# Attention and two MoE layers on one core: for the first batch, the softmax division moves behind the product with V

## The chip, the cores and the metric

The kernel runs on one core of one Trainium2 chip. The metric is the device time of one execution in microseconds; the time before is the median of three runs.

## What is computed

Four batches of eight heads of causal attention with a decay, 576 positions and 64 channels per head; then an MoE-like layer (a maximum over three products, and an output product), then a second one with a rational gate:

```python
scores = scale * np.matmul(q, k.transpose(0, 1, 3, 2))
scores = np.where(causal, -1000000000.0, scores + decay)
scores = scores - np.max(scores, axis=-1, keepdims=True)
attn = np.exp(scores)
attn = attn / (np.sum(attn, axis=-1, keepdims=True) + 1e-09)
x = np.matmul(attn, v)            # then heads side by side: (2304, 512)
h = np.maximum(np.maximum(x @ w1, x @ w2), x @ w3)
x2 = h @ w_out
...                               # second layer: x2 @ w_in, gate, @ w_out
```

The expert weights arrive as 64-bit floats and are turned into pairs of 32-bit halves (high and low) on the chip.

## The kernel before

Heads are handled two at a time: a `Pair` is two heads of one batch. The 576 queries are cut into five blocks (64, then four of 128) in two groups, g = 0 (the first 320 queries) and g = 1 (the last 256). The first batch is made of eight pairs, n = 0 to 3 for group 0 and n = 4 to 7 for group 1; from n = 8 on a pair has both groups. A `Unit` is one head and one group of a pair, and is named n_h_g: `e_7_1_1` is a tile of pair 7, head 1, group 1.

A unit goes through three steps of a software pipeline, one slot apart. In `scores` TensorE multiplies q and k (L343, or L345 and L346), VectorE adds the mask and takes the row maximum (L347), and ScalarE takes the exponential and its row sums (L353). `normalise` then adds 1e-9 to the sums and inverts them on VectorE (L358, L359), and GpSimd multiplies every block of probabilities by its reciprocal (L362). In `turn`, one slot later, TensorE transposes the probabilities (L382) and ScalarE copies them out of PSUM (L384). In `attend`, another slot later and once per pair, TensorE multiplies by V (L398); ScalarE and VectorE split the result into a high and a low part `x` (L405, L406).

The first MoE layer (`moe1_h`, L430 to L443, and `moe1_o`, L455 to L461) is cut into small pieces, which `fill` puts between the steps of the attention. A piece of `moe1_h` is twelve matmuls and one maximum `m`, whose tiles come from the pool `mpool` under the tag `mx`, which has three buffers. In the names, `h_0_0_4` is a product for batch 0, group 0, fourth chunk of channels counted from 0; `x2p` are the output products. The conversion of the weights (`convert`: L169 to L171 on ScalarE and VectorE, L172 and L175 on VectorE, L178 on ScalarE, L179 on GpSimd) is put in between by the same routine; it makes the tiles `cv_w`, `w1h`, `w1l` and their like. For the first four pairs TensorE also runs two matmuls on a constant before each use of a PSUM bank (`exercised`, L84).

A scheduler fixes the order on each engine when the program is built: it takes whatever its own model of the time holds ready, in the order in which the code was written. On the chip each engine runs its list in that order and waits where a semaphore says so.

Of the kernel before, what the change touches and what calls it, by code (L numbers as in the profile page):

```python
# [8 lines left out]
F32 = mybir.dt.float32  # L9
F32R = mybir.dt.float32r  # L10
I32 = mybir.dt.int32
AF = mybir.ActivationFunctionType
ALU = mybir.AluOpType
# [6 lines left out]
Q0 = [0, 64, 192, 320, 448]  # L20
# [4 lines left out]
GQ = [(0, 320), (320, 576)]  # L25
GBLK = [(0, 1, 2), (3, 4)]
# [6 lines left out]
GBANK = [[(1, 2), (0,)], [(1, 2), (3, 4), (0,)]]  # L33
# [4 lines left out]
def kernel(  # L38
    ctx: ExitStack, tc: tile.TileContext, q, k, v, f, w1, w2, w3, w_out, m2_in, m2_out, m2_a, m2_b, out
):  # L40
    nc = tc.nc
    B, H, S, D = q.shape
# [3 lines left out]
    P = 128  # L46
# [3 lines left out]
    NPAIR = H // 2  # L50
    NB = len(Q0)

    def r32(ap):
        return ap.bitcast(F32)
# [7 lines left out]
    mpool = ctx.enter_context(tc.tile_pool(name="mpool", bufs=1, side="left"))  # L62
    wpool = ctx.enter_context(tc.tile_pool(name="wpool", bufs=1, side="left"))
    apool_cm = ExitStack()
    apool = apool_cm.enter_context(tc.tile_pool(name="apool", bufs=1, side="right"))
    ps_cm = ExitStack()
    ps_s = ps_cm.enter_context(tc.tile_pool(name="ps_s", bufs=2, space=PSUM))
    ps_t = ps_cm.enter_context(tc.tile_pool(name="ps_t", bufs=3, space=PSUM))
# [4 lines left out]
    ident = const.tile([P, P], F32, name="ident")  # L73
# [6 lines left out]
    def exercised(bank, n):  # L80

        if n < 4:
            for _ in range(WARM):
                nc.tensor.matmul(bank, warm[:, 0], wide, start=True, stop=True)  # L84
        return bank
# [27 lines left out]


    LOOK, WHOLE, PRE = 2, 6, 2
    CONV2, EARLY = (32, 0.25), 12
    kqs = {}

# [105 lines left out]
    xt = {}  # L224
    x2d = dram.tile([P, NDC, 2, NT], F32R, name="x2d")

    def pinned(ld):
        tc.keep_in_program_order(ld)
# [12 lines left out]
    class Pair:  # L241


        def __init__(self, n, b, hp, groups):
            self.n, self.b, self.hp, self.groups = n, b, hp, groups
            self.ng = groups[-1] + 1
            self.nk = GBLK[groups[-1]][-1] + 1
            self.ik = [(2 * n + h) % NKB for h in range(2)]
            self.iq = [[(2 * n + h) % m for h in range(2)] for m in NQB]
            self.pt = {}  # L250
            self.whole = n < WHOLE
            self.iqf = [(2 * n + h) % 4 for h in range(2)]

        def load(self):
# [58 lines left out]
    class Unit:  # L313
# [5 lines left out]

        def begin(self):  # L320
            self.st = apool.tile([P, 9], F32, name=f"st_{self.nm}", tag="st", bufs=3)
            self.rs = apool.tile([P, 2, 3], F32, name=f"rs_{self.nm}", tag="rs", bufs=3)

        def scores(self, i):
            p, h, g = self.pair, self.h, self.g
# [29 lines left out]
        def normalise(self):  # L355
            blks = GBLK[self.g]
            n = len(blks)
            nc.vector.tensor_scalar_add(self.rs[:, 0, :n], self.rs[:, 0, :n], 1.0e-9)  # L358
            nc.vector.reciprocal(self.rs[:, 1, :n], self.rs[:, 0, :n])  # L359
            for j, i in enumerate(blks):  # L360
                e = self.e[i]
                nc.gpsimd.tensor_scalar(e, e, self.rs[:, 1, j : j + 1], 0.0, op0=ALU.mult, op1=ALU.add)  # L362

        def turn(self, bank):

            g, p = self.g, self.pair
            hi = GQ[g][1]
            if g not in p.pt:
                p.pt[g] = pts[g]
            pt = p.pt[g][:, self.h]  # L370
            chunks = GBANK[g][bank]
            tp = exercised(ps_t.tile([P, 512], F32, name=f"tp{bank}_{self.nm}", tag="t"), self.pair.n)
            base = GCH[g][chunks[0]][0]
            n = 0
            for c in chunks:
                col, q0 = GCH[g][c]
                kr = Q1[c] - Q0[c]
                for i in GBLK[g]:
                    if i < c:
                        continue  # L380
                    dst = col - base + Q0[i] - q0
                    nc.tensor.transpose(tp[:kr, dst : dst + P], self.e[i][:, Q0[c] : Q1[c]], ident)  # L382
                n += hi - q0
            nc.scalar.activation(pt[:kr, base : base + n], tp[:kr, :n], AF.Copy)  # L384

        def attend(self):

            p, h, g = self.pair, self.h, self.g
            if h == 0:
                return  # L390
            lo, hi = GQ[g]
            w = hi - lo
            ot = exercised(ps_o.tile([P, 512], F32, name=f"o_{self.nm}", tag="o"), p.n)
            order = list(GCH[g].items())
            with tc.high_priority():
                for j, (c, (col, q0)) in enumerate(order):
                    for i in (1, 0):
                        mm = nc.tensor.matmul(  # L398
                            ot[SIDES[i][0], q0 - lo : w], p.v[:, c, i], p.pt[g][:, i, col : col + hi - q0],
                            start=(j == 0), stop=(j == len(order) - 1),  # L400
                        )
                        if (j, i) != (0, 1):
                            pinned(mm)
            x = mpool.tile([P, 2, w], F32R, name=f"x_{self.nm}", tag=f"x{g}", bufs=(6, 8)[g])
            nc.scalar.activation(x[:, 0], ot[:, :w], AF.Copy)  # L405
            nc.vector.tensor_tensor(x[:, 1], ot[:, :w], r32(x[:, 0]), op=ALU.subtract)  # L406
            xt[p.b, p.hp, g] = x
# [131 lines left out]
    for step in range(len(slots) + 2):  # L539
        u = slots[step] if step < len(slots) else None  # L540
        t = slots[step - 1] if 0 <= step - 1 < len(slots) else None
        o = slots[step - 2] if 0 <= step - 2 < len(slots) else None
        prep, NPRE = [], 0
        if u is not None and u.pair.n + 1 < len(pairs):
            n = u.pair.n + 1
# [252 lines left out]
```

## Time and profile before

| | us |
|---|---|
| median of three runs (range) | 968.99 (967.96 to 969.51) |
| the profiled execution | 970.9 |
| its span, first to last instruction | 969.1 |

| engine | busy, us | share of the span |
|---|---|---|
| TensorE (PE) | 943.1 | 97% |
| weight loads (PEld) | 829.9 | 86% |
| VectorE (DVE) | 739.6 | 76% |
| ScalarE (ACT) | 623.8 | 64% |
| GpSimd (POOL) | 252.4 | 26% |

Shares are means over stages with different limits. The attention of the first batch takes the first 160 us; the conversion of the first layer's weights lies in the same stretch. A busy PE is not PE at its peak: the ends of matmuls are modelled, and a waiting matmul is partly counted. So the profile is read by stretches.

### The profile page before, as it was taken

Reading aid. Unit: us, or ns where it says so; the run is one execution under the profiler, and the core shown is the slowest. Engines: PE = TensorE matmul, PEld = TensorE weight load, DVE = VectorE, ACT = ScalarE, POOL = GpSimd, SP = SyncE. Lnnn points to the kernel's source line nnn. Section 1 sums busy time; section 2 is a strip of 40 time slices with the busy share of each in tenths; the row PEclk is TensorE's granted clock in tenths of the full one; section 3 lists DMA queues with packets and bytes.
Section 4 is the critical chain, followed back from the end, with each engine's and each line's share of the span. In section 5 each row is a group of like instructions: output and inputs, shape, how many; then the busy total and the mean of one; then the engine's idle time right before and its main releaser. Section 6 shows DMA issues by size and latency. Waiting matters only on the chain.

```text
span 969.1 us, 16846 instructions
## 1 busy us (share of the span) xinstructions
PE 943.1 (97%) x5780; PEld 829.9 (86%) x5780; DVE 739.6 (76%) x1756; ACT 623.8 (64%) x1457; POOL 252.4 (26%) x408
## 2 busy tenths in 40 slices
PE   7998999999999999999999999999999999999998
PEld 6767889998998988999999978888888888999997
DVE  5789985557777777534397949988888988899997
ACT  5875666667667666646454548767666766677775
POOL 2646553445454545425133400000000000000000
PEclk9978999999999999999999999999999999999999
DMA  6685233124446445230145477011002101100000
GB/s 160 159 236 153 64 83 89 43 63 119 140 131 205 133 136 174 58 94 1 57 140 185 132 253 269 1 44 43 1 1 66 44 1 46 64 1 1 34 1 33
DMA packets 125621, 88.52 MB, mean 91 GB/s; under 512 B 74448, under 2 KB 110304, under 8 KB 125536
## 3 DMA queue, kind: packets, MB, share of 16 engines
q1 hardware_dynamic: 125536, 87.45, 30.4%
q8 instruction: 46, 0.75, 0.4%
q14 instruction: 39, 0.32, 0.1%
HBM read 64.73 MB, written 22.69 MB: 90 GB/s over the span
## 4 chain that ended last, share of the span: by engine, by line
PE 70%; DVE 14%; DMA 6%; ACT 4%; issue 3%; POOL 2%; SPq 1%; ACTq 0%; POOLq 0%; DVEq 0%
PE oo L721 7%; PE oo L722 7%; PE oo L720 7%; PE hq L671 6%; PE hq L673 6%; PE hq L672 6%; PE tp L382 4%; PE h L430 4%; PE o L398 4%; PE h L431 4%; PE h L432 4%; PE x2p L455 2%; DMA raw_wi<-in_moe_w_in_dram 2%; PE x2p L456 2%; PE x2p L457 2%
## 5 line engine op out<-in xcount | busy, mean ns | idle before, releaser
L430 PE MATMUL h<-x,w1h 128*128 128x320 f32 (+1 forms) x576 | 176.6, 307 | 3.1 <-ACT m L435 2.2
L431 PE MATMUL h<-x,w1h 128*128 128x320 f32 (+1 forms) x576 | 172.1, 299 | 0.0
L432 PE MATMUL h<-x,w1l 128*128 128x320 f32 (+1 forms) x576 | 171.2, 298 | 0.0
L430 PEld LDWEIGHTS h<-x,w1h 128*128 128x128 f32 x576 | 109.4, 190 | 7.0 <-ACT m L435 3.0
L362 POOL TENSOR_SCALAR e<-e,rs 128x64 f32<-128x64 f32 (+4 forms) x160 | 87.7, 563 | 106.4 <-DVE rs L359 91.5
L353 ACT ACTIVATE e<-e,st 128x64 f32<-128x64 f32 (+4 forms) x160 | 89.1, 557 | 37.8 <-DVE st L347 36.0
L721 PE MATMUL oo<-wp,gh 128*128 128x512 f32 x288 | 112.9, 392 | 0.0
L720 PE MATMUL oo<-wp,gh 128*128 128x512 f32 x288 | 112.5, 390 | 0.0
L431 PEld LDWEIGHTS h<-x,w1h 128*128 128x128 f32 x576 | 109.5, 190 | 0.4 <-issue 0.2
L432 PEld LDWEIGHTS h<-x,w1l 128*128 128x128 f32 x576 | 109.2, 190 | 0.0
L722 PE MATMUL oo<-wp,gl 128*128 128x512 f32 x288 | 108.8, 392 | 0.0
L680 ACT ACTIVATE s<-hq 128x512 f32<-128x512 f32 (+1 forms) x80 | 44.3, 554 | 97.4 <-PE hq L673 97.4
L347 DVE CUSTOM_DVE_ANT_0 e<-s,mask 128x320 f32<-128x320 f32 (+3 forms) x160 | 67.2, 433 | 37.9 <-PE s L346 24.0
L384 ACT ACTIVATE pt<-tp 128x384 f32<-128x384 f32 (+3 forms) x160 | 69.8, 469 | 19.2 <-PE tp L382 17.4
L683 DVE SCALAR_TENSOR_TENSOR s<-s,ab,u 128x512 f32<-128x512 f32 (+1 forms) x80 | 55.7, 697 | 32.1 <-ACT u L681 31.9
L382 PE MATMUL tp<-ident,e 128*128 128x128 f32 (+1 forms) x480 | 78.0, 280 | 1.3 <-DVE k2s L275 0.6
L673 PE MATMUL hq<-x,wil 128*128 128x512 f32 (+1 forms) x192 | 70.4, 367 | 0.0
L671 PE MATMUL hq<-x,wih 128*128 128x512 f32 (+1 forms) x192 | 70.4, 367 | 0.0
L672 PE MATMUL hq<-x,wih 128*128 128x512 f32 (+1 forms) x192 | 70.3, 366 | 0.0
L722 PEld LDWEIGHTS oo<-wp,gl 128*128 128x128 f32 x288 | 54.1, 188 | 11.7
L720 PEld LDWEIGHTS oo<-wp,gh 128*128 128x128 f32 x288 | 54.2, 188 | 11.0
L721 PEld LDWEIGHTS oo<-wp,gh 128*128 128x128 f32 x288 | 54.1, 188 | 10.9
(129 smaller groups left out, 2433.6 us busy)
## 6 DMA issues: line engine op xcount, KB each, us to landing
raw_w<-in_moe_w_dram SPq DMA_DIRECT2D x18, 512.0 KB
raw_wp<-in_moe_w_out_dram SPq DMA_DIRECT2D x32, 256.0 KB
wpd<-wp SPq DMA_DIRECT2D x32, 256.0 KB
raw_wi<-in_moe_w_in_dram SPq DMA_DIRECT2D x32, 256.0 KB
wp<-wpd SPq DMA_DIRECT2D x10, 768.0 KB
x2d<-xo SPq DMA_DIRECT2D x16, 320.0 KB
out_dram<-ob SPq DMA_DIRECT2D x18, 256.0 KB
kn<-in_k_dram SPq DMA_DIRECT2D x32, 128.0 KB
```

Source lines behind the costliest of these rows:

```text
L353: nc.scalar.activation(e[:nr], e[:nr], AF.Exp, bias=m, scale=-1.0, accum_out=l)
L362: nc.gpsimd.tensor_scalar(e, e, self.rs[:, 1, j : j + 1], 0.0, op0=ALU.mult, op1=ALU.add)
L382: nc.tensor.transpose(tp[:kr, dst : dst + P], self.e[i][:, Q0[c] : Q1[c]], ident)
L430: nc.tensor.matmul(hp_[:, :w], wh[:, j, dc], xs[dc][:, 1], start=(dc == NDC - 1), stop=False)
L431: nc.tensor.matmul(hp_[:, :w], wh[:, j, dc], xs[dc][:, 0], start=False, stop=False)
L432: nc.tensor.matmul(hp_[:, :w], wl[:, j, dc], xs[dc][:, 0], start=False, stop=(dc == 0))
L671: nc.tensor.matmul(hp_[:, :w], wih[:, dc, fs], xh, start=(dc == 0), stop=False)
L672: nc.tensor.matmul(hp_[:, :w], wih[:, dc, fs], xl, start=False, stop=False)
L673: nc.tensor.matmul(hp_[:, :w], wil[:, dc, fs], xh, start=False, stop=(dc == NDC - 1))
L720: nc.tensor.matmul(o, g[0][:, ts_], wh_, start=(fc == 0), stop=False)
L721: nc.tensor.matmul(o, g[0][:, ts_], wl_, start=False, stop=False)
L722: nc.tensor.matmul(o, g[1][:, ts_], wh_, start=False, stop=(fc == NF2 - 1))
```

## The change

For the pairs of the first batch (n < `LATE`, which is 8) `normalise` no longer touches the probabilities. After the second head of a pair it adds 1e-9 and inverts the sums of both heads at once, and one GpSimd instruction spreads the reciprocals over a tile `rx` (64 equal columns per head and block). At the end of `turn` TensorE transposes `rx` block by block into a PSUM tile `rb`, and ScalarE copies that to `rn`, so that the reciprocals lie along the columns of the output. `attend` multiplies the output by `rn` on VectorE, and splits the product instead of the output itself. `rx` takes buffers of `e` tiles that the group doesn't use; `rn` takes a buffer of the tag `mx`.

```diff
+    LATE = NPAIR * 2
...
+            if self.pair.late:
+                if self.h == 1:
+                    rs = self.pair.rs
+                    nc.vector.tensor_scalar_add(rs[:, 0, :, :n], rs[:, 0, :, :n], 1.0e-9)
+                    nc.vector.reciprocal(rs[:, 1, :, :n], rs[:, 0, :, :n])
+                    rx = apool.tile([P, n, 2, D], F32, name=f"rx_{self.nm}", tag=("e3_", "e2_")[self.g] + str(self.pair.hp % 2))
+                    self.pair.rx = rx
+                    r = rs[:, 1, :, :n].rearrange("p h j -> p j h").unsqueeze(3).to_broadcast([P, n, 2, D])
+                    nc.gpsimd.tensor_scalar(rx, r, 1.0, 0.0, op0=ALU.mult, op1=ALU.add)
+                return
             nc.vector.tensor_scalar_add(self.rs[:, 0, :n], self.rs[:, 0, :n], 1.0e-9)
...
             nc.scalar.activation(pt[:kr, base : base + n], tp[:kr, :n], AF.Copy)
+            if p.late and self.h == 1 and bank == len(GBANK[g]) - 1:
+                lo, w = GQ[g][0], GQ[g][1] - GQ[g][0]
+                rb = ps_t.tile([P, 512], F32, name=f"rb_{self.nm}", tag="t")
+                for j, i in enumerate(GBLK[g]):
+                    nc.tensor.transpose(
+                        rb[:, Q0[i] - lo : Q0[i] - lo + P], p.rx[:, j].rearrange("p h d -> p (h d)"), ident
+                    )
+                p.rb = mpool.tile([P, 320], F32, name=f"rn_{self.nm}", tag="mx", bufs=3)
+                nc.scalar.activation(p.rb[:, :w], rb[:, :w], AF.Copy)
...
+            if p.late:
+                xn = p.rb
+                nc.vector.tensor_tensor(xn[:, :w], ot[:, :w], xn[:, :w], op=ALU.mult)
+                nc.scalar.activation(x[:, 0], xn[:, :w], AF.Copy)
+                nc.vector.tensor_tensor(x[:, 1], xn[:, :w], r32(x[:, 0]), op=ALU.subtract)
+                return
             nc.scalar.activation(x[:, 0], ot[:, :w], AF.Copy)
```

The new instructions give the scheduler another order. Two places show it. The first is TensorE's list around the unit 7_0_1 (`s` are score matmuls, `h` those of the first layer, `o` the product with V). Before, the last piece of the chunk `h_0_0_4` ends just ahead of the first scores of that unit:

```order
L431 MATMUL h_0_0_4_1805<-x_1_0_516,w1h_852 128x320
L432 MATMUL h_0_0_4_1805<-x_1_0_516,w1l_853 128x320
L430 MATMUL h_0_0_4_1805<-x_1_0_369,w1h_852 128x320
L431 MATMUL h_0_0_4_1805<-x_1_0_369,w1h_852 128x320
L432 MATMUL h_0_0_4_1805<-x_1_0_369,w1l_853 128x320
L345 MATMUL s_0_7_0_1_1483<-k1s_1334,q1s_1401 128x448
L346 MATMUL s_0_7_0_1_1483<-k2s_1335,q2s_1402 128x448
```

In the changed kernel the second piece of the same chunk begins only behind the scores of 8_1_0, the transposes `rb` of pair 7 and its product with V, with the scores of 8_0_1 begun:

```order
L407 MATMUL rb_1_1_1671<-ident,rx_1_1_1642 128x128 x2
L353 MATMUL s_0_8_1_0_1774<-k1s_1089,q1s_1625 128x320
L354 MATMUL s_0_8_1_0_1774<-k2s_1090,q2s_1626 128x320
L425 MATMUL o_1_1_1719<-pt_124,v_1422 64x256 x8
L425 MATMUL o_1_1_1719<-pt_124,v_1422 64x128 x2
L353 MATMUL s_0_8_0_1_1851<-k1s_1084,q1s_1153 128x448
L354 MATMUL s_0_8_0_1_1851<-k2s_1085,q2s_1154 128x448
L464 MATMUL h_0_0_4_1779<-x_1_0_836,w1h_848 128x320
```

So the pieces of the first layer stand later among the attention: ahead of the first scores of unit 8_1_1 there are 306 of its matmuls before (216 `h` of group 0, 72 `x2p`, 18 `h` of group 1) and 192 after. All other matmuls ahead of that place are the same in number, but for the 20 added transposes. Ahead of the scores of 13_0_0 the first layer's matmuls are again equal in number.

The second place is GpSimd's list in group 1. Before, each unit has two instructions on the probabilities between the low halves of the weights:

```order
L179 TENSOR_TENSOR w1l_674<-cv_w_2_675,w1h_673 128x512
L362 TENSOR_SCALAR e_4_0_1_783<-e_4_0_1_783,rs_0_1_782 128x448
L362 TENSOR_SCALAR e_4_0_1_798<-e_4_0_1_798,rs_0_1_782 128x576
L179 TENSOR_TENSOR w1l_674<-cv_w_2_708,w1h_673 128x512
L179 TENSOR_TENSOR w1l_674<-cv_w_2_725,w1h_673 128x512
L362 TENSOR_SCALAR e_4_1_1_888<-e_4_1_1_888,rs_1_1_887 128x448
L362 TENSOR_SCALAR e_4_1_1_903<-e_4_1_1_903,rs_1_1_887 128x576
L179 TENSOR_TENSOR w1l_752<-cv_w_3_753,w1h_751 128x512
```

In the changed kernel one instruction on the reciprocals stands for both units of a pair:

```order
L180 TENSOR_TENSOR w1l_669<-cv_w_2_702,w1h_668 128x512
L180 TENSOR_TENSOR w1l_669<-cv_w_2_719,w1h_668 128x512
L180 TENSOR_TENSOR w1l_745<-cv_w_3_746,w1h_744 128x512
L374 TENSOR_SCALAR rx_1_1_933<-rs_0_1_781 128x256
L180 TENSOR_TENSOR w1l_745<-cv_w_3_789,w1h_744 128x512
L180 TENSOR_TENSOR w1l_745<-cv_w_3_812,w1h_744 128x512
L374 TENSOR_SCALAR rx_1_1_1172<-rs_0_1_990 128x256
```

In the whole first batch 40 GpSimd instructions go and 8 come.

## Rows read from the trace of the kernel before

**Rows 1.** Windows: stretch, length, busy by engine (instructions), granted clock, DMA share, GB/s.

```profile
24.00:53.00 29.00, 28.49 (x166) 21.66 (x167) 20.19 (x66) 24.06 (x69) 17.20 (x24) 1.00 0.63 159
53.00:97.00 44.00, 38.99 (x196) 29.05 (x195) 41.24 (x86) 27.98 (x65) 25.62 (x25) 0.81 0.70 199
97.00:143.00 46.00, 41.27 (x287) 37.03 (x286) 42.37 (x111) 30.75 (x80) 26.66 (x38) 0.98 0.26 66
143.00:161.00 18.00, 18.00 (x125) 16.90 (x125) 7.82 (x31) 9.90 (x29) 4.79 (x12) 0.87 0.38 111
161.00:253.00 92.00, 90.92 (x738) 83.04 (x737) 55.93 (x206) 64.83 (x190) 43.34 (x84) 1.00 0.32 82
```

**Rows 2.** Timeline of VectorE around unit 8_1_1: start, duration, instruction.

```profile
155.41 0.42 DVE L406 TENSOR_TENSOR x<-o,x 128x256 fp32r<-128x256 f32 x1 [0.85 <-ACT x L405]
...
160.70 0.61 DVE L347 CUSTOM_DVE_ANT_0 e<-s,mask 128x448 f32<-128x448 f32 x1
```

**Rows 3.** Timeline of TensorE: two of the first layer's matmuls in a row.

```profile
79.81 0.31 PE L430 MATMUL h<-x,w1h 128*128 128x320 f32 x1
79.95 0.31 PE L431 MATMUL h<-x,w1h 128*128 128x320 f32 x1
```

**Rows 4.** Windows of line 362 alone: stretch, length, GpSimd busy (instructions), clock, DMA.

```profile
53.00:97.00 44.00, 6.67 (x8) 0.81 0.70 199
97.00:143.00 46.00, 6.00 (x8) 0.98 0.26 66
```

**Rows 5.** Groups by form, VectorE, 53 to 143 us: count, busy us, mean ns, idle before.

```profile
L175 DVE SCALAR_TENSOR_TENSOR cv_w<-raw_w,cv_w 128x512 int32<-128x512 int32 x12 | 11.4, 953 | 0.1
L172 DVE SCALAR_TENSOR_TENSOR cv_w<-raw_w,cv_w 128x512 int32<-128x512 int32 x12 | 9.8, 819 | 0.2
L175 DVE SCALAR_TENSOR_TENSOR cv_wo<-raw_wo,cv_wo 128x256 int32<-128x256 int32 x12 | 7.0, 586 | 0.2
...
L172 DVE SCALAR_TENSOR_TENSOR cv_wo<-raw_wo,cv_wo 128x256 int32<-128x256 int32 x12 | 6.0, 510 | 0.1
...
L170 DVE TENSOR_SCALAR cv_wo<-cv_wo 128x256 f32<-128x256 f32 x12 | 5.3, 448 | 0.8 <-ACT cv_wo L169 0.8
L171 DVE TENSOR_SCALAR cv_wo<-cv_wo 128x256 int32<-128x256 int32 x12 | 5.0, 426 | 0.1
```

**Rows 6.** Timeline of VectorE: the same forms where GpSimd stands still.

```profile
59.81 0.68 DVE L172 SCALAR_TENSOR_TENSOR cv_w<-raw_w,cv_w 128x512 int32<-128x512 int32 x1
...
113.91 0.42 DVE L175 SCALAR_TENSOR_TENSOR cv_wo<-raw_wo,cv_wo 128x256 int32<-128x256 int32 x1
114.25 0.28 DVE L170 TENSOR_SCALAR cv_wo<-cv_wo 128x256 f32<-128x256 f32 x1
114.57 0.29 DVE L171 TENSOR_SCALAR cv_wo<-cv_wo 128x256 int32<-128x256 int32 x1
```

**Rows 7.** Timelines of VectorE and of GpSimd at 58 us.

```profile
58.33 1.56 DVE L175 SCALAR_TENSOR_TENSOR cv_w<-raw_w,cv_w 128x512 int32<-128x512 int32 x1
...
58.06 1.27 POOL L179 TENSOR_TENSOR w1l<-cv_w,w1h 128x512 fp32r<-128x512 f32 x1 [5.44 <-ACT w1h L178]
```

**Rows 8.** Timelines of VectorE and of GpSimd at 28 us.

```profile
28.83 0.49 DVE L406 TENSOR_TENSOR x<-o,x 128x320 fp32r<-128x320 f32 x1
...
27.38 2.54 POOL L179 TENSOR_TENSOR w1l<-cv_w,w1h 128x512 fp32r<-128x512 f32 x2
```

**Rows 9.** Timeline of TensorE: three transposes and what follows them.

```profile
33.74 0.49 PE L297 MATMUL tk<-ident,kn 128*128 128x128 f32 x3
33.99 0.71 PE L84 MATMUL s<-warm 128*128 128x512 f32 x2
```

**Rows 10.** Windows, columns as in rows 1: the stretch around 230 us.

```profile
218.00:242.00 24.00, 22.92 (x177) 20.32 (x176) 16.80 (x59) 17.97 (x57) 12.17 (x22) 1.00 0.45 121
```

**Rows 11.** Product with V twice: TensorE's timeline at 74 us, the chain of waits at 152 us.

```profile
74.17 4.11 PE L398 MATMUL o<-pt,v 128*64 128x256 f32 x20 [0.83 <-DVE x L406]
...
152.85 2.10 PE o L398 x20
```

More of the change, by code (lines that the diff above doesn't have):

```diff
@@ L251, in __init__ @@
             self.whole = n < WHOLE
+            self.late = n < LATE
             self.iqf = [(2 * n + h) % 4 for h in range(2)]
@@ L321, in begin @@
             self.st = apool.tile([P, 9], F32, name=f"st_{self.nm}", tag="st", bufs=3)
-            self.rs = apool.tile([P, 2, 3], F32, name=f"rs_{self.nm}", tag="rs", bufs=3)
+            p = self.pair
+            if not p.late:
+                self.rs = apool.tile([P, 2, 3], F32, name=f"rs_{self.nm}", tag="rs", bufs=3)
+                return
+            if self.h == 0:
+                p.rs = apool.tile([P, 2, 2, 3], F32, name=f"rs_{self.nm}", tag="rsd", bufs=2)
+            self.rs = p.rs[:, :, self.h]
         def scores(self, i):
@@ L404, in attend @@
             x = mpool.tile([P, 2, w], F32R, name=f"x_{self.nm}", tag=f"x{g}", bufs=(6, 8)[g])
+            xt[p.b, p.hp, g] = x
+            if p.late:
[3 more added lines that the diff above has]
+                nc.vector.tensor_tensor(x[:, 1], xn[:, :w], r32(x[:, 0]), op=ALU.subtract)
+                return
             nc.scalar.activation(x[:, 0], ot[:, :w], AF.Copy)
```

## The prediction

> **What bounds the kernel now.** I read the windows by stage first [rows 1], then who is idle in each. From 24 to 53 us TensorE is busy 28.49 of 29 us and VectorE only 20.19: there the pairs of the first batch run at TensorE's pace, the constant matmuls of L84 included, and taking work off GpSimd or VectorE buys nothing. From 53 to 143 us it is the other way round. VectorE is busy 41.24 of 44 and 42.37 of 46 us, because the weights are converted there; TensorE has gaps, and its granted clock is 0.81 in the first of the two stretches, so part of that stretch ran at 1.2 GHz, not 2.4. From 143 to 161 us TensorE is busy 18.00 of 18 us and VectorE 7.82: now VectorE waits. From 161 us on TensorE is busy to within about a hundredth. So in the first 143 us VectorE decides from 53 us on, and later the amount of work that TensorE still has to do.
>
> That gives the way to count. I take as a mark the first score reduction of unit 8_1_1, at 160.70 us [rows 2]. From there on TensorE bounds, and by the scores of 13_0_0 both orders have done the same pieces of the first layer. The change in the total is the change in the time of the mark, plus the matmuls that the new order still owes at the mark, less idle time of TensorE that these owed matmuls fill afterwards.
>
> **The change part by part.**
>
> *Work on VectorE ahead of the mark.* The counts of the two orders differ there as follows. Eight multiplications with the reciprocals come: four of 320 columns at 0.49 us [rows 8] (the same shapes from PSUM) and four of 256 at 0.42 [rows 2], 3.6 us. Of the small additions and reciprocals, 30 become 16; at an estimated 0.16 us each, from the smallest VectorE operation that stands unstretched (0.28 for 256 columns [rows 6]) taken down for their few columns, that is 2.3 us less. Six operations of the first layer (two maxima, four splits) now stand behind the mark, and they have the shape of L406 at 0.49 us [rows 8]: 3.0 us less. Together -1.7 us. The conversions ahead of the mark are the same in number.
>
> *GpSimd's share of the stretching.* VectorE's conversions are slower beside GpSimd. At 58.33 us an L175 lasted 1.56 us while GpSimd's L179 ran from 58.06 for 1.27 [rows 7]; alone such a form takes 0.68 [rows 6] (L172 of the same shape). Over 53 to 143 us the excess is, as the means of rows 5 less the single times of rows 6 [rows 5, 6]: 12 x (0.953 - 0.68) = 3.3 and 12 x (0.819 - 0.68) = 1.7 for the large ones, 12 x (0.586 - 0.42) = 2.0, 12 x (0.510 - 0.42) = 1.1, 12 x (0.448 - 0.28) = 2.0 and 12 x (0.426 - 0.29) = 1.6 for the small ones, 11.7 us in all. GpSimd is busy 25.62 + 26.66 = 52.3 us there [rows 1], of which L362 has 12.7 [rows 4]; five of the new instructions come in, at an estimated 0.6 us each (L362 has 0.8 us for its mean of 512 columns [rows 4], and they have 256 or 384), 3 us. So 9.7 of 52.3 us go, 18.5%, and with them 18.5% of the excess: -2.2 us. The bounds are 0 (the rest of GpSimd's work moves up and stands in the way instead) and -9.7 (all of it was in VectorE's way). The value is near the first, since most of the stretching stands beside L179, which stays.
>
> *VectorE's idle time before the mark.* From 143 to 161 us VectorE idles 10.2 us behind TensorE [rows 1]. TensorE owes less there in the new order, so most of this closes: 54 of the first layer's matmuls stand between the scores of 8_0_0 and of 8_1_1 before, 36 after, while VectorE has some 3 us of work more between the two. I take -7.5 us; the bounds are -3 (the latency of score, maximum, exponential and transpose stays) and -10.2.
>
> The mark then comes at 160.7 - 1.7 - 2.2 - 7.5 = 149.3 us.
>
> *What TensorE owes at the mark.* 306 less 192 is 114 matmuls of 128x320, which follow each other every 0.147 us (79.81, 79.95 and on [rows 3]): +16.8 us. They are on the path, because TensorE has no idle time to speak of from 143 us on. This is the largest term. It comes from `rn`: it takes its turn in the three `mx` buffers, and a later maximum of the first layer gets that buffer only when the pair's output is split. Before, the first layer ran ahead of the attention and filled TensorE while VectorE converted weights; now it cannot run ahead.
>
> *Added transposes.* Three take 33.99 - 33.74 = 0.25 us [rows 9]. Nine fall into the stretch to 53 us where TensorE bounds: +0.7 us. The other eleven lie under VectorE's time; without that cover they would cost 0.9 us. ScalarE's two added copies per pair are covered as well: it is busy 27.98 of 44 us [rows 1]. A transpose `rb` makes TensorE wait for GpSimd, as the transposes of the probabilities did; queued behind it are the next scores and the product with V. `rx` sits in buffers of `e` tiles: the third block of 8_1_0 waits for the `rb` of pair 7, which stands just ahead of it.
>
> *Idle time of TensorE that fills.* Around 230 us, where only attention is left, TensorE idles 1.1 us [rows 10]; in the new order pieces of the first layer stand there: -1.1 us, from 0 to -3.4 with the 4.7 us that ran at the lower clock between 143 and 161 us (0.87 of 18 us [rows 1]), worth half their length, 2.3 us.
>
> Sum: -1.7 - 2.2 - 7.5 + 16.8 + 0.7 - 1.1 = **+5.0 us**. The profiled execution's span of 969.1 us becomes 974.1, its time of 970.9 some 975.9; on the median of 968.99 us that is **974.0 us**.
>
> **The rivals.**
>
> *VectorE gains more than TensorE loses (faster).* The division leaves the way from the exponential to the transposes, and the attention needs neither GpSimd nor the small VectorE operations in between. If the stretching goes by 7.5 us, the idle time by 10.2 and another 3 us of the 6.4 that VectorE idles between 53 and 143 us [rows 1], the sum is -1.7 - 7.5 - 10.2 - 3 + 16.8 + 0.7 - 1.1 = -6.0 us, 963.0 us. It decides from a mark at 144.4 us on. For it speaks that VectorE bounds this very stretch; against it that the conversions stay and that L179 is most of the stretching. Chance 0.27.
>
> *A wash.* The work removed was off the path and the owed matmuls mostly find room: mark near 144 us, within 0.2% of 969 us. The change then does what it says to no end. Chance 0.18.
>
> *The clock stays low for longer (slower still).* With the first layer gone from 100 to 145 us TensorE has fewer matmuls there, and before it was in such a stretch, with scores and transposes alone, that the clock fell: the product with V took 4.11 us at 74 us against 2.10 later [rows 11]. Some 16 us of matmuls at half speed take 16 more, of which VectorE's time hides half: +5 + 8 = +13, 982 us. Chance 0.08.
>
> *The new split collides with GpSimd.* L406 beside L179 kept its 0.49 us [rows 8]; its operands are one tile in PSUM and one in SBUF. The new subtraction reads two tiles in SBUF, like L175 [rows 7]. If each of the eight is stretched in proportion, by up to (1.56 - 0.68) for 52.3 of the 90 us, the eight cost 4 us, about 3 of them on the path: 977 us. By the Trainium skill (SBUF — State Buffer, section "Who interferes with whom") a VectorE instruction with two inputs in SBUF contends with a GpSimd instruction that reads SBUF, and one with at most one such input does not; the trace agrees in both rows. Chance 0.05 by itself.
>
> **How the numbers follow.** The forecast itself has 0.42, and its own range is 969.5 to 980. Slower by over 0.2% (1.9 us, about what a measurement of this kernel can tell from no change): 0.42 + 0.08 + 0.05 = 0.55; within: 0.18; faster: 0.27. The lower end of the range is the faster rival's 963.0. The upper end has no relief at GpSimd, 3 us of idle time closed, nothing filled later and 3 us for the clock: -1.7 - 3 + 16.8 + 0.7 + 3 = +15.8, cut to 984.5.
>
> **What would show each step.** GpSimd's busy time before 161 us falls by some 20 us. The VectorE reduction of 8_1_1 comes near 149 us; past 155 the idle time did not close, before 144.4 the faster rival has it. Between 97 and 150 us TensorE's busy share falls, and from the mark to 253 us it is full, with no dip around 230. A granted clock well under 0.98 between 97 and 143 us would show the clock rival. L175 and L172 keep means over 0.8 us in any case. I am wrong if TensorE has as many of the first layer's matmuls done at 160 us as before.

## The result and the profile after

The changed kernel takes 975.7 us in the median (974.68 to 977.18, four runs) against 969.25 us for the kernel before beside it (967.96 to 969.55): a ratio of 1.0070, interval 1.0053 to 1.0088. It is slower by 0.7%, and 974.0 had been forecast. The profiled execution after has a span of 972.9 us and a time of 974.7 us, the lowest of its four, so the two traces are 3.8 us apart where the medians are 6.5.

The same windows as in [rows 1], of the changed kernel (stretch, length, busy by engine, granted clock, DMA share, GB/s):

```profile
24.00:53.00 29.00, 27.68 (x164) 21.03 (x161) 21.59 (x61) 22.95 (x65) 9.85 (x8) 1.00 0.54 141
53.00:97.00 44.00, 39.83 (x229) 30.53 (x229) 41.77 (x93) 33.56 (x81) 19.42 (x20) 0.92 0.76 212
97.00:143.00 46.00, 38.59 (x226) 30.07 (x225) 41.35 (x121) 32.03 (x90) 22.11 (x36) 0.81 0.30 74
143.00:161.00 18.00, 18.00 (x135) 17.16 (x134) 10.16 (x35) 11.46 (x31) 9.96 (x18) 1.00 0.24 54
161.00:253.00 92.00, 92.00 (x748) 85.58 (x747) 50.61 (x181) 58.93 (x171) 36.37 (x71) 1.00 0.29 80
```

Between 97 and 143 us TensorE is busy 2.7 us less than before, with 226 matmuls instead of 287, while VectorE is still busy 41.35 of 46 us; from 143 to 253 us TensorE has no idle time at all. The low clock has changed its places: 0.92 and 0.81 now stand where 0.81 and 0.98 stood, and 1.00 where 0.87 stood. The granted clock is either full or half (2.4 or 1.2 GHz), so a mean of 0.81 over 46 us holds 2 x 0.19 x 46 = 17.5 us at half clock. So counted, from 53 to 161 us the kernel before has 16.7 + 1.8 + 4.7 = 23.2 us, the changed one 7.0 + 17.5 = 24.5. The clock is given to 0.01, so such a sum is good to about 1 us; in one window from 53 to 161 us both kernels have a mean of 0.89.

The marks of the prediction, in VectorE's timeline: the first score reduction of units 4_0_1, 8_1_1 and 13_0_0. Before they stood at 53.62, at 160.70 [rows 2] and at 261.66 us:

```profile
53.62 0.62 DVE L347 CUSTOM_DVE_ANT_0 e<-s,mask 128x448 f32<-128x448 f32 x1
...
261.66 0.23 DVE L347 CUSTOM_DVE_ANT_0 e<-s,mask 128x64 f32<-128x64 f32 x1
```

In the changed kernel:

```profile
56.40 0.58 DVE L355 CUSTOM_DVE_ANT_0 e<-s,mask 128x448 f32<-128x448 f32 x1
...
150.15 0.61 DVE L355 CUSTOM_DVE_ANT_0 e<-s,mask 128x448 f32<-128x448 f32 x1
...
266.77 0.20 DVE L355 CUSTOM_DVE_ANT_0 e<-s,mask 128x64 f32<-128x64 f32 x1
```

8_1_1 comes 10.55 us earlier, and 13_0_0, by which both orders have done the same pieces of the first layer, 5.1 us later. The 15.66 us between the two shifts are what TensorE owed at the first of these two marks, less the idle time that the owed work filled. The dip of [rows 10] is gone:

```profile
218.00:242.00 24.00, 24.00 (x199) 22.28 (x198) 12.51 (x46) 14.73 (x42) 9.08 (x19) 1.00 0.41 113
```

GpSimd's groups to 161 us (L380 is the multiplication that was L362, now for batch 1 alone) in the changed kernel:

```profile
L374 POOL TENSOR_SCALAR rx<-rs 128x384 f32<-128x384 f32 (+1 forms) x8 | 4.6, 570 | 14.8 <-DVE rs L370 13.8 <-PE tp L400 1.1
L380 POOL TENSOR_SCALAR e<-e,rs 128x64 f32<-128x64 f32 (+4 forms) x10 | 5.6, 571 | 0.6 <-DVE rs L377 0.3
```

Its busy time in one window to 161 us, of the kernel before:

```profile
0.00:161.00 161.00, 79.41 (x113) 0.93 0.51 138
```

and of the changed one:

```profile
0.00:161.00 161.00, 64.56 (x92) 0.93 0.50 134
```

It lost 14.9 us there, not the 20 of the prediction: with the earlier mark, more of the work behind it falls into the window. Counted in each kernel up to its own mark at 8_1_1, the time falls from 79.41 to 58.65 us, by 20.8:

```profile
0.00:160.70 160.70, 79.41 (x113) 0.93 0.51 138
```

and of the changed kernel:

```profile
0.00:150.15 150.15, 58.65 (x81) 0.92 0.52 139
```

VectorE's conversions in the changed kernel from 53 to 143 us, by form (count, busy us, mean ns), to be read against [rows 5]:

```profile
L176 DVE SCALAR_TENSOR_TENSOR cv_w<-raw_w,cv_w 128x512 int32<-128x512 int32 x12 | 10.3, 860 | 0.0
L173 DVE SCALAR_TENSOR_TENSOR cv_w<-raw_w,cv_w 128x512 int32<-128x512 int32 x12 | 10.1, 845 | 0.2
L172 DVE TENSOR_SCALAR cv_w<-cv_w 128x512 int32<-128x512 int32 x12 | 8.5, 708 | 0.1
L173 DVE SCALAR_TENSOR_TENSOR cv_wo<-raw_wo,cv_wo 128x256 int32<-128x256 int32 x12 | 7.4, 619 | 0.2
L171 DVE TENSOR_SCALAR cv_w<-cv_w 128x512 f32<-128x512 f32 x12 | 6.4, 536 | 0.8 <-ACT cv_w L170 0.8
...
L176 DVE SCALAR_TENSOR_TENSOR cv_wo<-raw_wo,cv_wo 128x256 int32<-128x256 int32 x12 | 5.2, 432 | 0.1
L172 DVE TENSOR_SCALAR cv_wo<-cv_wo 128x256 int32<-128x256 int32 x12 | 4.4, 366 | 0.2
...
L171 DVE TENSOR_SCALAR cv_wo<-cv_wo 128x256 f32<-128x256 f32 x12 | 3.8, 317 | 1.2 <-ACT cv_wo L170 1.1
```

Eight groups, 56.1 us for 96 instructions; before it was 57.0 us for 95 (the two groups that [rows 5] leaves out, L171 and L170 of `cv_w`, have 6.4 and 6.1 us). The stretching moved from one form to another and shrank by about 1.4 us, since the one instruction more would by itself have added about 0.5.

### The profile page after: what moved, and what is told of

Same layout as the page of the kernel before. It is cut to its first block, busy times and chain, and to the rows that moved or that the text cites. A ratio compares the mean times of both kernels' runs of the same rounds, so it can differ in the third digit from the quotient of the medians.

```text
span 972.9 us, 16833 instructions
## 1 busy us (share of the span) xinstructions
PE 945.9 (97%) x5800; PEld 830.9 (85%) x5800; DVE 739.3 (76%) x1748; ACT 628.5 (65%) x1465; POOL 231.4 (24%) x376
## 4 chain that ended last, share of the span: by engine, by line
PE 74%; DVE 15%; DMA 5%; ACT 3%; issue 2%; POOL 1%; SPq 1%; ACTq 0%; DVEq 0%; POOLq 0%
PE oo L755 7%; PE oo L756 7%; PE oo L754 7%; PE hq L705 6%; PE hq L707 6%; PE hq L706 6%; PE o L425 5%; PE h L464 5%; PE h L466 4%; PE h L465 4%; PE tp L400 4%; PE x2p L489 2%; PE s L354 2%; PE s L353 2%; PE x2p L491 2%
## 5 line engine op out<-in xcount | busy, mean ns | idle before, releaser
L464 PE MATMUL h<-x,w1h 128*128 128x320 f32 (+1 forms) x576 | 175.9, 305 | 1.1 <-DVE m L471 0.9
L464 PEld LDWEIGHTS h<-x,w1h 128*128 128x128 f32 x576 | 109.1, 189 | 3.3 <-DVE m L471 2.0
L380 POOL TENSOR_SCALAR e<-e,rs 128x448 f32<-128x448 f32 (+3 forms) x120 | 64.2, 550 | 71.0 <-DVE rs L377 63.4
L400 PEld LDWEIGHTS tp<-ident,e 128*128 128x128 f32 (+1 forms) x480 | 56.3, 135 | 9.8 <-issue 2.2
L754 PEld LDWEIGHTS oo<-wp,gh 128*128 128x128 f32 x288 | 54.1, 188 | 11.1
```

Source lines behind the costliest of these rows:

```text
L464: nc.tensor.matmul(hp_[:, :w], wh[:, j, dc], xs[dc][:, 1], start=(dc == NDC - 1), stop=False)
L754: nc.tensor.matmul(o, g[0][:, ts_], wh_, start=(fc == 0), stop=False)
```

## The experiments

Twelve kernels were run. Ratios are to the kernel before run beside them (966.8 to 968.3 us in the median, and 969.25 beside the change); a gain or loss in us that is said to go by ratios is the ratio's share of 967 us. "Half clock" is worked out from each kernel's windows from 53 to 161 us, as above, and good to about 1 us; the marks are first score reductions in VectorE's timeline.

| kernel | ratio (interval) | median, us | half clock, us | 4_0_1 | 8_1_1 | 13_0_0 |
|---|---|---|---|---|---|---|
| before | 1 | 968.3, 967.2, 967.1, 966.8 | 23.2 | 53.62 | 160.70 | 261.66 |
| the change | 1.0070 (1.0053 to 1.0088) | 975.7 | 24.5 | 56.40 | 150.15 | 266.77 |
| ring_alone | 1.0065 (1.0042 to 1.0087) | 974.4 | 27.2 | 52.81 | 153.80 | 267.22 |
| rn_free | 1.0046 (1.0027 to 1.0065) | 972.5 | 20.5 | 56.46 | 162.77 | 266.22 |
| late_ring_undone | 1.0041 (1.0029 to 1.0054) | 971.0 | 13.6 | 55.70 | 152.46 | 263.84 |
| hi_free | 0.9971 (0.9957 to 0.9984) | 965.4 | 17.6 | 53.17 | 153.18 | 260.99 |
| hi_ring | 1.0041 (1.0026 to 1.0056) | 970.7 | 20.1 | 53.05 | 151.85 | 265.07 |
| lo_free | 1.0025 (1.0011 to 1.0040) | 969.3 | 10.7 | 55.93 | 158.94 | 260.73 |
| no_division | 0.9878 (0.9855 to 0.9900) | 956.7 | 7.0 | 56.48 | 145.27 | 252.16 |
| no_division_late | 0.9876 (0.9856 to 0.9896) | 954.9 | 7.0 | 53.41 | 144.54 | 251.01 |
| no_division_early | 0.9986 (0.9973 to 0.9998) | 965.5 | 14.1 | 56.41 | 154.26 | 259.79 |
| warm_before | 1.0036 (1.0015 to 1.0057) | 971.0 | 7.0 | 54.55 | 164.54 | 264.36 |
| warm_after | 1.0114 (1.0096 to 1.0131) | 978.0 | 3.7 | 57.06 | 153.56 | 269.45 |
| hi_paced | 0.9964 (0.9947 to 0.9980) | 963.7 | 10.1 | 53.26 | 148.63 | 254.98 |

Where an expectation counts conversions, it counts their instructions on VectorE, four to a conversion.

### The ring alone

```diff
             nc.scalar.activation(pt[:kr, base : base + n], tp[:kr, :n], AF.Copy)
+            if p.n < 8 and self.h == 1 and bank == len(GBANK[g]) - 1:
+                p.rb = mpool.tile([P, 320], F32, name=f"rn_{self.nm}", tag="mx", bufs=3)
+                nc.scalar.activation(p.rb[:64, :1], tp[:64, :1], AF.Copy)
...
             nc.vector.tensor_tensor(x[:, 1], ot[:, :w], r32(x[:, 0]), op=ALU.subtract)
+            if p.n < 8:
+                nc.vector.tensor_scalar_add(p.rb[:64, :1], p.rb[:64, :1], 1.0)
```

> The kernel before with the ring alone: for each of the first eight pairs a tile of tag mx is taken in turn and given back after the split, with a one-column ScalarE copy and a one-column VectorE addition to hold it; the division stays where it was. 197 matmuls of the first layer stand ahead of unit 8_1_1, 109 fewer than before: 16.0 us owed. Ring theory: the mark closes most of VectorE's idle time (10.2 us between 143 and 161 us), so it comes at 150 to 154 us, and the whole is 973 to 979 us. Rival (the ring is harmless): 968 to 971 us.

It took 974.4 us, 6.3 us more than before, with the division left as it was: the ring theory's case. Holding a buffer of `mx` per pair, with the two one-column instructions that hold it, is enough for a loss of the size of the whole change. Its windows show the shape of the changed kernel's: TensorE is busy 37.69 us between 97 and 143 us (41.27 before) and full after it, while VectorE has even less room.

```profile
53.00:97.00 44.00, 35.33 (x192) 27.11 (x191) 41.85 (x89) 28.28 (x67) 25.90 (x25) 0.89 0.67 193
97.00:143.00 46.00, 37.69 (x232) 30.70 (x232) 43.16 (x124) 32.57 (x95) 28.03 (x41) 0.81 0.29 73
```

### The ring undone in the changed kernel

```diff
+    rnt = []
...
-                p.rb = mpool.tile([P, 320], F32, name=f"rn_{self.nm}", tag="mx", bufs=3)
+                if not rnt:
+                    rnt.append(mpool.tile([P, 2, 320], F32, name="rn", tag="x0", bufs=6))
+                p.rb = rnt[0][:, p.n % 2]
```

> The changed kernel with one thing undone: rn no longer takes a buffer of the tag mx; the reciprocals of all eight pairs lie in the two halves of one tile under the tag x0, which nothing else wants at that time. In the order of TensorE 309 matmuls of the first layer then stand ahead of unit 8_1_1, as before (306), against 192 in the changed kernel. Ring theory (the first layer cannot run ahead, and that is the loss): the 16.8 us owed at the mark are gone, the mark comes at 156 to 161 us, and the whole takes 963 to 969 us, 0.6 to 1.3% less than the changed kernel. Rival (the ring is harmless; the loss is the 3 us by which the first four pairs come later, 46.33 against 43.35 us for pair 3, carried to the end): it stays at 973 to 977 us.

It took 972.5 us. Both theories missed, the ring theory's 963 to 969 by more: freeing the ring gave back only some 2.3 us of 6.8 by ratios, and as the two intervals overlap, even that is not clear of noise. The trace says where the rest stands. The first layer did run ahead again, but 7_0_1 came at 134.23 us (121.08 in the changed kernel): VectorE ran some thirty instructions of w_out conversions between 121 and 134 us, and the scores stood behind them. TensorE had little to do there, and its clock fell. Windows of rn_free:

```profile
120.00:124.00 4.00, 2.99 (x19) 2.55 (x17) 2.88 (x10) 2.69 (x7) 1.09 (x2) 1.00 0.00 1
124.00:128.00 4.00, 1.10 (x5) 0.60 (x5) 4.00 (x11) 1.75 (x5) 2.11 (x3) 0.79 0.21 66
128.00:132.00 4.00, 3.12 (x10) 2.62 (x10) 4.00 (x10) 1.91 (x6) 2.40 (x3) 0.50 0.39 128
```

So one edit at a buffer's tag had also re-dealt the conversions. late_ring_undone was made to leave the order up to 6_1_1 alone:

```diff
+    rnt = []
...
-                p.rb = mpool.tile([P, 320], F32, name=f"rn_{self.nm}", tag="mx", bufs=3)
+                if p.n < 4:
+                    p.rb = mpool.tile([P, 320], F32, name=f"rn_{self.nm}", tag="mx", bufs=3)
+                else:
+                    if not rnt:
+                        rnt.append(mpool.tile([P, 2, 320], F32, name="rn", tag="x0", bufs=6))
+                    p.rb = rnt[0][:, p.n % 2]
```

> The changed kernel with rn of pairs 4 to 7 alone outside the tag mx (pairs 0 to 3, which are done before the first layer begins, still take its buffers). Unlike rn_free this leaves the order up to unit 6_1_1 nearly as in the changed kernel: 95 conversions ahead of unit 7_0_1 on VectorE as there, where rn_free had 103 and a row of w_out conversions in one piece. 258 matmuls of the first layer stand ahead of unit 8_1_1 (192 in the changed kernel, 306 before). Ring theory (the ring costs 6 to 7 us, as ring_alone and hi_ring against hi_free show, and rn_free lost part of that again to its row of conversions): 967 to 971 us. Rival (rn_free was right, the ring is worth 2.5 us in the changed kernel): 972 to 975 us.

971.0 us, at the upper edge of the ring theory's case; as ratios, 1.0041 against 1.0070, the ring is worth 0.29% or 2.8 us here, with intervals that just touch. The row of conversions, which this kernel does not have, therefore does not explain why the ring is worth less in the full change than alone.

### Pairs 4 to 7, and pairs 0 to 3, by themselves

```diff
-        self.late = n < LATE
+        self.late = 4 <= n < LATE
```

hi_ring is the changed kernel with this line; hi_free has rn outside the ring too.

> As the kernel with rn outside the ring, but only pairs 4 to 7 divide late; pairs 0 to 3 are as before the change. 267 matmuls of the first layer stand ahead of unit 8_1_1 (306 before): 39 x 0.147 = 5.7 us owed at the mark. Ring theory: the mark comes some 6 to 9 us earlier than 160.7, as VectorE's idle time closes, and the whole is 966 to 970 us. Rival (the loss is in the first four pairs, whose rx and rb are new on TensorE's way there): without them 964 to 967 us, at least 4 us below the kernel with all eight pairs late and rn outside the ring.

> The changed kernel with the late division for pairs 4 to 7 alone, and rn in the tag mx as in the change; pairs 0 to 3 are as before the change. Beside hi_free (965.4 us) it differs by the ring alone: 196 matmuls of the first layer stand ahead of unit 8_1_1 instead of 267. Ring theory (the ring costs some 6 us wherever it is, as ring_alone showed): 970 to 973 us, and beside the changed kernel it lacks the late start of the first four pairs. Rival (the ring costs what it costs by the clock's low stretches, which fall as they fall): its time follows its half-clock time, 965 us at 17 us of it, 969 at 25.

hi_free took 965.4 us, faster than both kernels. That is the range of the rival, which puts the loss into the first four pairs, and 7.1 us below rn_free as it wanted; lo_free, below, speaks against it. hi_ring took 970.7, inside the ring theory's 970 to 973; by its half clock the rival had given some 967. The ring costs 0.70%, 6.8 us, between these two. One of the first layer's three matmul lines shows what it holds back (the other two lines have as many again each). L464 of hi_ring between 97 and 161 us:

```profile
97.00:143.00 46.00, 9.43 (x28) 0.82 0.30 77
143.00:161.00 18.00, 5.11 (x16) 1.00 0.20 46
```

The same line of hi_free, L467 there:

```profile
97.00:143.00 46.00, 12.22 (x39) 0.92 0.28 73
143.00:161.00 18.00, 0.92 (x3) 0.91 0.38 111
```

```diff
-    LATE = NPAIR * 2
+    LATE = 4
```

> Only pairs 0 to 3 divide late, with rn outside the ring; pairs 4 to 7 are as before the change. Theory that the first four pairs pay (TensorE sets their pace, 12 transposes of rx come in there, and waits for rx): the 2 to 3 us of delay at pair 4 stay, and the whole is 971 to 976 us, some 4 to 7 over the kernel before, as rn_free against hi_free says. Rival (the two halves interact, and the 7 us between rn_free and hi_free come from the low-clock stretches between 126 and 147 us): 966 to 970 us.

969.3 us, 2.4 us over before by the ratio: inside the rival's range, below the theory's. The delay at 4_0_1 is there (55.93 us), but the added transposes are not the whole of it: no_division_early, which has no transposes of rx at all, has 56.41. In all of these kernels most of the delay already stands on TensorE, where the first score matmuls of that unit begin. TensorE's timelines of the kernel before, the changed kernel, lo_free and no_division_early, in this order:

```profile
52.34 1.46 PE L343 MATMUL s<-kf,qf 66*128 66x448 f32 x4
...
54.79 1.46 PE L351 MATMUL s<-kf,qf 66*128 66x448 f32 x4
...
54.32 1.46 PE L352 MATMUL s<-kf,qf 66*128 66x448 f32 x4
...
54.30 0.92 PE L343 MATMUL s<-kf,qf 66*128 66x448 f32 x2
```

Ahead of the mark TensorE has, in the changed kernel and in lo_free, nine transposes `rb` and three matmuls on the constant more than before; in no_division_early it has four transposes of probabilities and five matmuls on the constant more, which only stand earlier in its order. On VectorE four to six more instructions of conversions stand ahead of 4_0_1, and the reduction follows the start of its matmuls by 1.6 to 2.1 us instead of 1.3. So part of the delay is work brought forward; how much, no run shows. The added transposes in this stretch are one short row, TensorE's window of their line from 24 to 56 us in the changed kernel (six of the nine):

```profile
24.00:56.00 32.00, 1.04 (x6) 1.00 0.57 144
```

### What the division had cost

```diff
+            if self.pair.n < 8:
+                return
             nc.vector.tensor_scalar_add(self.rs[:, 0, :n], self.rs[:, 0, :n], 1.0e-9)
```

no_division has these lines; the other two have `4 <= self.pair.n < 8` and `self.pair.n < 4` in them.

> The kernel before with the division of the first batch left out altogether (no 1e-9, no reciprocal, no multiplication on GpSimd for pairs 0 to 7; its attention outputs are not divided). It prices what the change takes away, without what it adds. 270 matmuls stand ahead of unit 8_1_1: 36 x 0.147 = 5.3 us owed. By the terms of the sum: -2.2 us of stretching, 30 small VectorE instructions at 0.16 us = -4.8, idle time that closes -3 to -7: 960 to 966 us. Rival (the removed work was off the path): 968 to 970 us.

> The kernel before with the division left out for pairs 4 to 7 alone (their attention outputs are not divided). Theory that the division cost where VectorE bounds, in pairs 4 to 7: 957 to 961 us, most of the 11.6 us of no_division. Rival (the 11.6 us are the clock's, 17 us less at half clock, and come whole or not at all): the time follows the half-clock time, some 966 us if that stays near 20 us. Against hi_free (965.4 us) the difference is the price of what the change adds for these four pairs.

> The kernel before with the division left out for pairs 0 to 3 alone (their attention outputs are not divided). Theory that TensorE sets the pace of the first four pairs, so that nothing is won there: 967 to 970 us. Rival (earlier conversions, 80 instead of 66 of them ahead of unit 6_0_1, win time later): 960 to 965 us. Against lo_free (969.3 us, 2.0 over its kernel before) the difference is the price of what the change adds for the first four pairs.

956.7, 954.9 and 965.5 us. The first two are below every range that was given for them, and the third lies between its two. The division of pairs 4 to 7 had cost 12 us, that of pairs 0 to 3 some 1.4, and together they cost no more than the first alone. Windows of no_division_late, again to be held against [rows 1]:

```profile
53.00:97.00 44.00, 39.17 (x243) 30.47 (x242) 41.99 (x92) 33.49 (x79) 19.66 (x19) 0.92 0.69 197
97.00:143.00 46.00, 42.64 (x303) 38.90 (x302) 38.46 (x113) 31.31 (x89) 25.29 (x38) 1.00 0.35 93
143.00:161.00 18.00, 18.00 (x148) 17.13 (x146) 10.46 (x38) 13.07 (x37) 8.04 (x16) 1.00 0.28 76
```

16 us less at half clock can be worth up to 8 us of the 12: this is the clock rival's account. It is not the whole of it, since no_division_early loses 9 us of half clock and gains 1.4 us.

### Constant matmuls against the low clock

```diff
-        if n < 4:
-            for _ in range(WARM):
+        if n < 8:
+            for _ in range(WARM if n < 4 else 1):
```

> The kernel before with one matmul on the constant ahead of each use of a PSUM bank for pairs 4 to 7 too: 64 matmuls of 512 columns more, 64 x 0.23 = 14.7 us of TensorE's time, order of the rest nearly the same. Clock theory (the 24 us at half clock, 62 to 79 and 141 to 148 us, hold the kernel up by up to half their length, and TensorE's idle time in that stretch takes the added matmuls): the half-clock time falls below 8 us and the whole takes 957 to 966 us. Rival (TensorE's low clock is hidden by VectorE's conversions, and the added matmuls come on top): 970 to 983 us.

> The changed kernel with the same 64 added matmuls on the constant for pairs 4 to 7. Clock theory: its half-clock time (24 us, as before the change) falls below 8 us and the whole takes 962 to 971 us; what is then left against warm_before, 3 to 7 us, is the change without the clock. If the change's loss came through the clock alone, the two are within 1.5 us. Rival (matmuls on top): 977 to 990 us.

The clock did what was wanted, 7.0 and 3.7 us at half clock instead of 23.2 and 24.5, and both kernels became slower, by 3.5 and 4.3 us. Both times lie in the rival's range. In the kernel before, the 16.2 us saved at half clock are worth at most half their length, 8.1; the added matmuls take 14.7 (64 at 0.23 us, an estimate from their spacing in the trace), so of these TensorE's idle time took at least some 3. The two kernels stay 7.5 us apart, so with the clock at full speed in nearly the whole stretch in both, the change's loss is still there: it does not come through the clock.

```profile
53.00:97.00 44.00, 41.00 (x224) 31.78 (x222) 42.68 (x86) 29.30 (x66) 22.85 (x21) 0.92 0.69 192
97.00:143.00 46.00, 42.73 (x278) 36.65 (x279) 41.59 (x105) 28.00 (x73) 27.02 (x38) 1.00 0.25 67
```

These are windows of warm_before: VectorE is still busy 42.68 of 44 and 41.59 of 46 us, and in the second stretch TensorE, at 42.73, has no more room than VectorE.

### Conversions a little later

On top of the edits of hi_free:

```diff
-        state["c"] += 0.15 if step < 7 else 0.5
+        state["c"] += 0.15 if step < 8 else 0.5
```

> As hi_free (late division in pairs 4 to 7, rn outside the ring), with the conversions of the first layer's weights written a little later: the slower pace of the first seven slots holds for eight. Between units 5_1_1, 6_0_1, 7_0_1 and 8_0_0 VectorE then has 20, 26 and 32 of them (hi_free: 27, 21 and 25; no_division_late, the fastest so far: 20, 31 and 24). Theory (what hi_free loses against no_division_late, 9 us, is where conversions stand in a row ahead of the scores, so that TensorE idles and its clock falls, 136 to 146 us in hi_free): with the second low stretch gone the whole takes 955 to 962 us. Rival (the 9 us are the price of the added transposes, copies and multiplications themselves): 963 to 968 us.

963.7 us, in the rival's range, with single runs from 961.39 to 966.44 (the profiled one is the lowest). The second low stretch did not go, so the theory's condition was not met and its claim is not decided. hi_free and hi_paced are both below the kernel before, and their intervals overlap. The windows of hi_free from 132 to 140 us show the pattern of rn_free once more, TensorE busy for about a quarter of the time beside a full VectorE, and then the clock at half:

```profile
132.00:136.00 4.00, 1.12 (x6) 0.60 (x5) 3.97 (x8) 3.50 (x10) 3.66 (x7) 0.99 0.53 140
136.00:140.00 4.00, 3.62 (x14) 3.25 (x15) 3.81 (x14) 1.56 (x5) 2.71 (x5) 0.50 0.02 5
```

no_division_late has no such hole from 128 to 136 us:

```profile
128.00:136.00 8.00, 7.25 (x50) 6.47 (x49) 7.26 (x23) 4.95 (x15) 5.64 (x10) 1.00 0.22 49
```

## Why the prediction was right, step by step

**The way of counting** held. Mark 149.3 forecast, 150.15 measured; matmuls owed and refilled idle time 16.8 - 1.1 = 15.7 forecast, 15.66 measured between the two marks; +5.0 forecast at the end, +5.1 at 13_0_0, +3.8 in the spans and +6.5 in the medians. An agreement to a tenth of a microsecond is partly luck: the trace before is of an execution of 970.9 us, above all of the timed runs of that kernel beside it, and the trace after is of the lowest of its four. What the prediction named as the sign of being wrong did not come: TensorE's records hold 306 of the first layer's matmuls begun by 160 us before and 236 after.

**VectorE's work ahead of the mark**, with the stretching, was forecast at -1.7 - 2.2 = -3.9. From the start to the mark VectorE is busy 123.37 us before and 119.59 after, 3.8 less. VectorE's windows before:

```profile
0.00:160.70 160.70, 123.37 (x335) 0.93 0.51 138
```

and after:

```profile
0.00:150.15 150.15, 119.59 (x323) 0.92 0.52 139
```

The stretching between 53 and 143 us gave 1.4 of it rather than 2.2.

**Its idle time** to the mark fell from 160.70 - 123.37 = 37.3 to 150.15 - 119.59 = 30.6 us, by 6.8. The forecast had -7.5 for it and +0.7 for the transposes that TensorE adds ahead of the mark; the sum of the total has both, but the mark of 149.3 leaves the 0.7 out, and with it would have been 150.0. The 6.8 contain the delay of 2.8 us at 4_0_1, where the sum had only that 0.7. This was the term whose reason fell short: it counted the transposes (1.04 us of TensorE's time for six of them, measured to 56 us), but not the matmuls on the constant and the conversions that the new order puts ahead of 4_0_1. TensorE's first score matmuls of that unit begin 2.45 us later, and 1.96 later in no_division_early, which has no such transposes.

**The ring as the cause** is right in kind: ring_alone costs 6.3 us without any other part of the change, and hi_ring 6.8 over hi_free. That it makes the loss of the full change is not shown, since undoing it there gave back less than half. But the forecast took the change as a small gain and one large debt. The runs show larger parts. In pairs 4 to 7 alone, by ratios: taking the division out -12.0 us (no_division_late), putting the late form in +9.2 (hi_free), the ring +6.8 (hi_ring), and then pairs 0 to 3 +2.8 (the change): +6.8 in all. The terms for VectorE were thus too small on both sides, and it is by luck that they met near the right sum.

**The faster rival** had something real: without the ring and for pairs 4 to 7 alone the late division wins 2.8 us by the ratio. In the full change it was outweighed. Which part of it won is not shown, since VectorE's conversions were dealt anew there too.

**The clock rival**'s sign was badly chosen. It was to show as a clock well under 0.98 between 97 and 143 us; 0.81 came, yet the total at half clock hardly changed (23.2 and 24.5 us, which is about what such a sum is good to), because it left the neighbouring stretches. A sign for a clock has to be a total.

**The colliding subtraction**, held for 0.05, happened. VectorE's timeline of the changed kernel, four of the subtractions L437, and GpSimd's at the same times:

```profile
86.10 1.11 DVE L437 TENSOR_TENSOR x<-rn,x 128x256 fp32r<-128x256 f32 x1
110.93 0.86 DVE L437 TENSOR_TENSOR x<-rn,x 128x256 fp32r<-128x256 f32 x1
125.79 0.41 DVE L437 TENSOR_TENSOR x<-rn,x 128x256 fp32r<-128x256 f32 x1
...
143.03 0.93 DVE L437 TENSOR_TENSOR x<-rn,x 128x256 fp32r<-128x256 f32 x1
```

```profile
85.20 1.73 POOL L180 TENSOR_TENSOR w1l<-cv_w,w1h 128x512 fp32r<-128x512 f32 x1 [0.46 <-ACT w1h L179]
...
110.78 0.73 POOL L180 TENSOR_TENSOR wo<-cv_wo,wo 128x256 fp32r<-128x256 f32 x1
...
124.98 0.73 POOL L180 TENSOR_TENSOR wo<-cv_wo,wo 128x256 fp32r<-128x256 f32 x1 [1.27 <-ACT wo L179]
...
142.94 0.74 POOL L180 TENSOR_TENSOR wo<-cv_wo,wo 128x256 fp32r<-128x256 f32 x1 [1.25 <-ACT wo L179]
```

Three of the four lie on a GpSimd instruction and take 0.86 to 1.11 us; the one at 125.79 starts after GpSimd has ended and takes 0.41. The other four, of 320 columns, meet no GpSimd instruction and take 0.48 to 0.49. That is 1.7 us for the three, not the 4 of the rival, and the product L435, one of whose operands is in PSUM, took 0.41 to 0.49, the three of its eight that lie on a GpSimd instruction too. This agrees with what the Trainium skill (SBUF — State Buffer, section "Who interferes with whom") says of two inputs in SBUF. The other half of that rule, as the prediction has it, is too wide for this case: the conversions `TENSOR_SCALAR` of `cv_w` have one tile as input, and those of L172 took 708 ns in the mean between 53 and 143 us, where GpSimd is at work, but 0.42 us at 54.67 us, where it stands still.

**What stays open.** The ring is worth 6.3 and 6.8 us where pairs 0 to 3 are as before, and 2.3 to 2.8 us where they divide late (rn_free and late_ring_undone against the change), amounts that are hardly clear of noise. hi_free at -2.8 and lo_free at +2.4 make +4.5 together, not -0.4. Each edit re-deals some of the conversions on VectorE, and no run held that order fixed; how much of the 9.2 us between no_division_late and hi_free is the added instructions, and how much the holes that the new order leaves TensorE, is not settled.

## What to carry to other kernels

A scratch tile that borrows a buffer from another stage's ring ties the two stages together in program order; look at who stands next in that ring before counting what the moved work costs, and look for a ring whose next taker is far off (here a tile of `x0` in place of `mx` made the late division in pairs 4 to 7 a gain: hi_free against hi_ring). Where a scheduler deals the rest of the work anew after each edit, count at marks by which both orders have done the same work, and hold an effect of a few microseconds for a cause only when it shows beside two different neighbours. By these runs the moved division helped in pairs 4 to 7, where VectorE had the least room, and lost in pairs 0 to 3, where TensorE had; as the orders differed too, that is a lead and not a rule.

## What the runs showed of the hardware

The time that TensorE ran at half clock differed widely between the kernels, from 3.7 to 27.2 us of the same 108, but the total did not follow it: at 7.0 us of it warm_before took 971.0 us and no_division_late 954.9. In rn_free and hi_free its fall lies in or behind stretches of 4 us in which TensorE was busy for 1.10 and 1.12, behind VectorE's conversions. Constant matmuls kept the clock up and still lost, since half of the saved 16.2 us is less than the estimated 14.7 us that they took. A subtraction of two tiles in SBUF took 0.41 us beside an idle GpSimd and 0.86 to 1.11 us on top of a GpSimd instruction.
